# Expert weights of a soft mixture of experts: each lane loads neighbouring rows as one run of 8192 bytes, and slot inputs and ReLU results are turned from strided columns

## The chip, the core and the metric

The kernel runs on one core of a Trainium2 chip. The metric is the time of one execution on the device in microseconds (us). A core has five engines that run side by side and meet at semaphores: PE (TensorE, the matmuls; PEld is its weight load), DVE (VectorE), ACT (ScalarE), POOL (GpSimd) and SP (SyncE, which here issues nearly all transfers). The transfers themselves are carried by 16 DMA engines.

## The reference, cut to what matters

Attention with clusters comes first, then a soft mixture of eight experts (the part that is changed), then a feed-forward layer with a PReLU.

```python
def _moe_ref(x, phi, w1, w2):          # x 1536x512, w1 8x512x1024, w2 8x1024x512
    logits = x @ phi                   # 32 slots, four for each expert
    d = exp(logits - max over tokens); d /= d.sum(0) + 1e-9
    slot_input = (d.T @ x).reshape(8, 4, 512)
    for e in range(8):
        h = np.maximum(slot_input[e] @ w1[e], 0.0)      # 4x1024
        slot_out[e] = h @ w2[e]                         # 4x512
    ...
    return c @ slot_out
```

The feed-forward layer behind it is `prelu(x @ w_in) @ w_out`, with weights that arrive as 64-bit floats and are unpacked by ACT, DVE and POOL.

## The kernel before

**Stages.** From the start to about 270 us the kernel works on 16 heads of attention (lines 500 to 725: scores, exponentials, sums, products with v). Around 262 to 279 us the slots' inputs are formed (`dispatch`), from 279 to 311 us the eight experts run, and from 312 us to the end the feed-forward layer runs. An order written out by numbers (`TABLE`) decides in which order the steps of the attention are issued; the expert stage and what follows are written out as code. Each engine works through its own instructions in that order, and each transfer is issued by SP in its place in SP's order.

**Expert weights.** Each expert has four units of 1 MB: two of w1 (256 rows of 1024 floats each) and two of w2 (512 rows of 512 floats each), 32 units in all. A unit lies in one buffer of 128 lanes (partitions) by 2048 floats. `load_w` (line 239) issues the loads, all at line 248. Of units 0 to 19, which are loaded beside the attention, 18 are loaded in two halves (`half` 0 and 1) and units 15 and 19 whole; units 20 to 31 are loaded whole by `more_w`, three into `unit_we` and nine into `unit_wr`. Before the change lane p holds rows p, p+128, p+256 and so on of its unit: two runs of 4096 bytes for w1, four runs of 2048 bytes for w2.

**An expert.** `siT` holds the slots' inputs turned over (features in lanes, 32 slots in columns), made at lines 1030 to 1038: eight matmuls (four in the code, and each float32 matmul leaves two records in the trace) with a slice of `si` as stationary operand. `expert1(e)` (line 1095) multiplies `siT` with w1, 16 matmuls over 256 columns that give the 1024 hidden values as four strips of 32 lanes by 256 columns, and ACT writes them with a ReLU to `hs` (line 1105). `turn(e)` (line 1107) lets DVE turn each block of 32x32 of `hs` into `hT`, so that hidden values lie in lanes. `expert2(e)` (line 1112) multiplies `hT` with w2, eight matmuls over 512 columns. `hs` and `hT` have one buffer each, so `turn(e+1)` waits until `expert2(e)` has read `hT`. For e up to 5 the code issues `expert1(e+1)` ahead of `expert2(e)`; for e = 6 it comes behind it. `comb_step` puts four other pieces of work in between, and `warm` puts in small matmuls that compute nothing.

**Behind the experts.** The sum of the experts is turned (line 1224), multiplied with `w_in` (line 1243), and the layer's two products follow (lines 1280 and 1316 to 1318). `load_o` issues the loads of `w_out` (lines 1165 to 1174), and three parts of `w_in` come back from a scratch tensor `wsp` in DRAM (line 842), where they lie as runs of 8192 bytes for each lane.

Of the kernel before, what the change touches and what calls it, by code (L numbers as in the profile page):

```python
# [16 lines left out]
P = 128  # L17
# [97 lines left out]
def clustered_attention_soft_moe_prelu_ffn(  # L115
# [32 lines left out]
    pe, dve, act, pool, sp = nc.tensor, nc.vector, nc.scalar, nc.gpsimd, nc.sync  # L148
# [25 lines left out]
    def misc(dt=F32, hold=False):  # L174
        turns[0] = 1 - held[0] if held else 1 - turns[0]
        if hold:
            held.append(turns[0])
        return psm.tile([P, 1024 if dt == BF16 else 512], dt, name=f"misc{turns[0]}")
# [5 lines left out]
    def unit(pl, dt=F32):  # L184
        return pl.tile([P, 2048], dt, name=f"unit_{pl.name}")
# [51 lines left out]
    wts = {}  # L237

    def load_w(u, pl, half=None):
        e, i = divmod(u, 4)  # L240
        if half in (None, 0):
            wts[u] = unit(pl).rearrange("p (k f) -> p k f", k=2 if i < 2 else 4)
        t = wts[u]
        src = (w1[e, i * 256:i * 256 + 256] if i < 2 else w2[e, (i - 2) * 512:(i - 1) * 512])
        src = src.rearrange("(k p) f -> p k f", p=P)
        k = t.shape[1] // 2
        n = slice(0, 2 * k) if half is None else slice(half * k, half * k + k)
        sp.dma_start(out=t[:, n], in_=src[:, n])
# [68 lines left out]
    dsp = {}  # L317
# [526 lines left out]
    def more_w(n, pl):  # L844
        for _ in range(min(n, 32 - nxt[0])):
            load_w(nxt[0], pl)
            nxt[0] += 1
# [9 lines left out]
    for h in range(NH):  # L857
        s0, p = 6 * h, h // 2
        z = {0: "z_", NH - 1: "t_"}.get(h, "")
        ld = T["ld"][h] if h < len(T["ld"]) else 0  # L860
        for c in range(6):
# [3 lines left out]
            k = c if h == NH - 1 and c > 3 else c | 1  # L865
# [98 lines left out]
    def more_l(u, nm, half):  # L964
        if nm not in lf:
            refill(nm, *{"a": (2, early, opa), "b": (1, opb), "c": (1, opc)}[nm])
        load_w(u, lf[nm], half)
# [21 lines left out]
    for e in sorted(ev, key=lambda e: e[:2]):  # L989
        assert all(n in done or n in tags for n in e[4]), e  # L990
        wait.append(e)
        while True:
# [4 lines left out]
            _, _, f, a, need, tag = go  # L997
# [16 lines left out]
    siT = cp.tile([P, 4, 32], F32, name="siT")  # L1014
# [15 lines left out]
    for r in range(2):  # L1030
        ps = misc()
        l0 = r * 64
        for k in range(2):
            pe.matmul(
                ps[:, k * 32:k * 32 + 32], dsp["si"][l0:l0 + 64, k * P:k * P + P],
                G[l0:l0 + 64, :32], start=True, stop=True,
            )
        dve.tensor_copy(siT[:, 2 * r:2 * r + 2].rearrange("p k s -> p (k s)"), ps[:, :64])
# [55 lines left out]
    hTs = {}  # L1094
    def expert1(e):
        hp_ = ps1.tile([P, 2, 512], F32, name="s1")[:, 0, :256]
        for k in range(4):
            wa = wts[4 * e + k // 2][:, k % 2, :].rearrange("p (c f i) -> p f c i", c=8, f=4)
            for f in range(4):
                pe.matmul(  # L1100
                    hp_[f * 32:f * 32 + 32, :].rearrange("p (c i) -> p c i", c=8), siT[:, k, :],
                    wa[:, f], start=(k == 0), stop=(k == 3),
                )
        hTs[e] = hs = cp.tile([P, 256], F32, name="hs")
        act.activation(hs, hp_, AF.Relu, scale=cs[:, C_EM + e:C_EM + e + 1])

    def turn(e):
        hT = cp.tile([P, 256], F32, name="hT")
        dve.transpose(hT, hTs[e])
        hTs[e] = hT  # L1110

    def expert2(e):
# [11 lines left out]
    PIPE = T["pipe"]  # L1124
    WC, WD, WE = T["wc"]
    expert1(0)
    comb_step(0)
    more_w(2, wr)
    slopes()
    warm(wk[10])  # L1130
    turn(0)
    warm(wk[11])
    for e in range(8):
        if e < PIPE:
            expert1(e + 1)
        expert2(e)
        if PIPE <= e < 7:
            expert1(e + 1)
        if e < 7:
            turn(e + 1)  # L1140
        more_w(4, wr)
        if e in (3, 5, 6):
            comb_step((e - 1) // 2 if e < 6 else 3)
# [78 lines left out]
    ps = misc()  # L1222
# [211 lines left out]
```

## Time and profile before

| what | us |
|---|---|
| median of 3 runs | 473.07 |
| lowest and highest run | 467.2 and 473.77 |
| the profiled execution: its own time | 472.17 |
| its span, from first to last instruction | 470.4 |
| PE busy in the span | 440.7 (94%) |
| 16 DMA engines: share taken by SP's queue | 58.5% |

The span is shorter than the execution's own time by 1.8 us, which lie around it. All times in the rows below count from the span's start.

### The profile page before, as it was taken

To read this page: it belongs to the slowest core of one execution; us is meant where nothing else is said; L and a number is where in the kernel's file an instruction comes from. 1 tells how busy PE (TensorE), PEld (TensorE's weight loads), DVE (VectorE), ACT (ScalarE), POOL (GpSimd) and SP (SyncE) were. 2 spreads that over 40 slices of the span, in tenths; PEclk is the share of its full clock that TensorE was granted. 3 is DMA by queue.
4 is the path that set the end of the run, shared out by engine and by line. 5 is a ranking of instruction groups with operands and counts; after the bars stand their busy time and mean duration, and the time that the engine had idled before them with its cause. 6 is when DMAs were issued, how large, how long until landed. Compare 5 with 4: busy or idle time off the path is not lost.

```text
span 470.4 us, 8258 instructions
## 1 busy us (share of the span) xinstructions
PE 440.7 (94%) x2964; PEld 296.5 (63%) x2964; DVE 312.6 (66%) x527; ACT 289.7 (62%) x542; POOL 232.6 (49%) x277
## 2 busy tenths in 40 slices
PE   8879998999997999998999889988799999999996
PEld 5656555566564555664655444456588888888885
DVE  3777879978779477786561571337899996444442
ACT  4868597778767566685654311258898865343341
POOL 4547789878998488798988100013432330000000
PEclk9999999999999799999999999999999999999999
DMA  8796985587678559776688799998121003000003
GB/s 310 211 319 169 277 263 169 143 243 237 208 238 224 168 181 285 242 240 200 182 246 278 303 363 381 398 416 346 54 86 42 1 1 134 1 0 0 1 1 134
DMA packets 35357, 90.50 MB, mean 192 GB/s; under 512 B 5298, under 2 KB 5894, under 8 KB 34932
## 3 DMA queue, kind: packets, MB, share of 16 engines
q1 hardware_dynamic: 34884, 89.73, 58.5%
q8 instruction: 23, 0.38, 0.3%
q10 hardware_dynamic: 432, 0.24, 0.2%
q14 instruction: 18, 0.15, 0.1%
HBM read 69.57 MB, written 6.33 MB: 161 GB/s over the span
## 4 chain that ended last, share of the span: by engine, by line
PE 59%; DVE 13%; DMA 12%; issue 7%; ACT 5%; POOL 3%; SPq 1%; POOLq 0%; DVEq 0%; ACTq 0%
PE s L604 9%; PE ot L632 9%; PE ob L1317 8%; PE ob L1318 8%; PE ob L1316 8%; PE s L536 6%; DVE cs L543 4%; DMA unit_wr<-in_w_out 4%; DMA unit_wr<-in_w 3%; DMA B<-unit_wr 2%; PE hp L1280 2%; PE s L1100 1%; PE L L660 1%; ACT pt L607 1%; DMA B<-ohm 1%
## 5 line engine op out<-in xcount | busy, mean ns | idle before, releaser
L620 POOL TENSOR_TENSOR ss<-ss,pt 128x384 f32<-128x384 f32 x150 | 145.3, 1005 | 12.7 <-PE ot L632 12.5
L543 DVE TENSOR_REDUCE cs<-s 128x1 f32<-128x768 f32 x93 | 88.5, 951 | 41.9 <-PE s L536 41.5
L607 ACT ACTIVATE pt<-s 128x384 f32<-128x384 f32 x160 | 70.0, 489 | 51.3 <-PE s L604 48.9
L604 PE MATMUL s<-A,B 97*128 97x384 f32 (+1 forms) x384 | 94.9, 368 | 5.0 <-DMA B<-unit_wr 2.5
L604 PEld LDWEIGHTS s<-A,B 97*128 97x128 f32 (+1 forms) x384 | 64.3, 193 | 33.6 <-issue 17.3
L1316 PE MATMUL ob<-unit_wr,gh 128*128 128x512 f32 x192 | 75.6, 394 | 1.7 <-ACT unit_wr L1342 1.2
L1317 PE MATMUL ob<-unit_wr,gh 128*128 128x512 f32 x192 | 75.1, 391 | 1.7 <-POOL unit_wr L1208 1.7
L1318 PE MATMUL ob<-unit_wr,gl 128*128 128x512 f32 x192 | 75.1, 391 | 0.0
L1208 POOL TENSOR_TENSOR unit_wr<-unit_wr 128x256 fp32r<-128x256 f32 x32 | 24.9, 801 | 86.2 <-ACT unit_wr L1201 83.7
L632 PE MATMUL ot<-pt,raw_v 128*64 128x384 f32 x320 | 63.1, 507 | 0.0
L536 PE MATMUL s<-B,A 96*128 96x384 f32 x192 | 53.9, 363 | 7.2 <-DVE cs L543 4.9
L1302 DVE SCALAR_TENSOR_TENSOR g<-hp,sal,hs 128x768 f32<-128x768 f32 (+1 forms) x34 | 32.8, 968 | 27.4 <-ACT hs L1300 27.3
L1300 ACT ACTIVATE hs<-hp,sgn 128x768 f32<-128x768 f32 (+1 forms) x34 | 29.1, 861 | 27.0 <-PE hp L1280 26.7
L536 PEld LDWEIGHTS s<-B,A 96*128 96x128 f32 x192 | 32.7, 192 | 19.8 <-DVE cs L543 16.2
L1316 PEld LDWEIGHTS ob<-unit_wr,gh 128*128 128x128 f32 x192 | 36.0, 188 | 9.1 <-ACT unit_wr L1342 1.6
L1317 PEld LDWEIGHTS ob<-unit_wr,gh 128*128 128x128 f32 x192 | 36.1, 188 | 8.7 <-POOL unit_wr L1208 2.4
L1318 PEld LDWEIGHTS ob<-unit_wr,gl 128*128 128x128 f32 x192 | 36.1, 188 | 8.1 <-DVE gl L1306 0.3
L1306 DVE TENSOR_TENSOR gl<-g,gh 128x768 fp32r<-128x768 f32 (+1 forms) x34 | 30.8, 911 | 15.4 <-ACT gh L1304 15.3
L1304 ACT ACTIVATE gh<-g 128x768 fp32r<-128x768 f32 (+1 forms) x34 | 27.3, 805 | 18.3 <-DVE g L1302 18.1
L632 PEld LDWEIGHTS ot<-pt,raw_v 128*64 128x64 f32 x320 | 20.0, 138 | 24.0 <-issue 23.3
L698 POOL TENSOR_TENSOR unit_wr<-unit_wr,tr 128x192 f32<-128x192 f32 x13 | 7.7, 593 | 34.6 <-DVE tr L696 34.6
L797 POOL TENSOR_TENSOR unit_wr<-unit_wr 128x256 uint32<-128x256 uint32 x32 | 22.5, 730 | 2.8 <-DVE unit_wr L790 2.8
(198 smaller groups left out, 611.8 us busy)
## 6 DMA issues: line engine op xcount, KB each, us to landing
unit_wr<-in_w SPq DMA_DIRECT2D x30, 512.0 KB
unit_wr<-in_w SPq DMA_DIRECT2D x9, 1024.0 KB
unit_wr<-in_w_in SPq DMA_DIRECT2D x16, 512.0 KB
unit_wr<-in_w_out SPq DMA_DIRECT2D x5, 1024.0 KB
unit_wr<-in_qn SPq DMA_DIRECT2D x8, 384.0 KB
unit_wr<-in_qT SPq DMA_DIRECT2D x8, 384.0 KB
unit_wr<-in_kn SPq DMA_DIRECT2D x8, 384.0 KB
unit_wr<-in_kT SPq DMA_DIRECT2D x8, 384.0 KB
```

The costliest lines, as they stand in the source:

```text
L536: pe.matmul(ps[hf], a[:96, c * P:c * P + P], b[:96, hf * 384:hf * 384 + 384], start=True, stop=True,)
L543: dve.tensor_reduce(m, t, axis=AX.XY, op=ALU.max, negate=True)
L604: pe.matmul(ps[:, :384], b[:, c * P:c * P + P], a[:, hs], start=(i == 0), stop=(i == 1))
L607: act.activation(e[:, hs], ps[:, :384], AF.Exp, scale=0.125)
L620: (pool if h < T["sp"] else dve).tensor_tensor(ss[h][:, hs], ss[h][:, hs], sme[h, c][:, hs], op=ALU.add)
L632: pe.matmul(ot[h][hf * 64:hf * 64 + 64, :], v[:, c, par * 64:par * 64 + 64], e[:, hf * 384:hf * 384 + 384], start=(c == 0), stop=(c == 5),)
L1300: act.activation(hs, hv, AF.Copy, scale=sgn[:, f:f + 1])
L1302: dve.scalar_tensor_tensor(g, hv, sal[:, f:f + 1], hs, op0=ALU.mult, op1=ALU.max)
L1306: dve.tensor_tensor(gl, g, gh.bitcast(F32), op=ALU.subtract)
L1316: pe.matmul(ob[t], gh[:, c], wh(f), start=(f == 0), stop=False)
L1317: pe.matmul(ob[t], gh[:, c], wlo(f), start=False, stop=False)
L1318: pe.matmul(ob[t], gl[:, c], wh(f), start=False, stop=(f == 15))
```

## The change

Lane p now takes neighbouring rows: rows 2p and 2p+1 of a unit of w1, rows 4p to 4p+3 of a unit of w2. A whole unit is then one run of 8192 bytes in each lane. A half keeps a run of 4096 bytes for w1 and gets one of 4096 bytes, in place of two of 2048, for w2. The features that lie in lane p are thereby others, so two operands are reordered to match: the slice of `si` that makes `siT` takes every second column (`k:k + 255:2`) in place of 128 neighbouring ones, and `turn` reads `hs` in each 32x32 block with a step of four floats (16 bytes) and writes `hT` as before. The view of w1 in `expert1` has two runs of 128 columns for each matmul in place of eight runs of 32.

```diff
@@ load_w @@
         src = (w1[e, i * 256:i * 256 + 256] if i < 2 else w2[e, (i - 2) * 512:(i - 1) * 512])
-        src = src.rearrange("(k p) f -> p k f", p=P)
+        src = src.rearrange("(p k) f -> p k f", p=P)
@@ siT @@
-                ps[:, k * 32:k * 32 + 32], dsp["si"][l0:l0 + 64, k * P:k * P + P],
+                ps[:, k * 32:k * 32 + 32], dsp["si"][l0:l0 + 64, k:k + 255:2],
@@ expert1 @@
-            wa = wts[4 * e + k // 2][:, k % 2, :].rearrange("p (c f i) -> p f c i", c=8, f=4)
+            wa = wts[4 * e + k // 2][:, k % 2, :].rearrange("p (c f i) -> p f c i", c=2, f=4)
             for f in range(4):
                 pe.matmul(
-                    hp_[f * 32:f * 32 + 32, :].rearrange("p (c i) -> p c i", c=8), siT[:, k, :],
+                    hp_[f * 32:f * 32 + 32, :].rearrange("p (c i) -> p c i", c=2), siT[:, k, :],
                     wa[:, f], start=(k == 0), stop=(k == 3),
@@ turn @@
-        dve.transpose(hT, hTs[e])
+        dve.transpose(
+            hT.rearrange("p (c g s) -> p c g s", c=2, g=4),
+            hTs[e].rearrange("p (c i g) -> p c g i", c=2, g=4),
+        )
```

No instruction is added, removed or moved on any engine; only the shapes of transfers and operands differ. The place where this shows is SP's list of transfers at the end of the attention and in the expert stage. In the rows, `unit_wr`, `unit_wc` and `unit_we` are buffers of weight units by their pools, `in_w` is w1 or w2, `in_w_out` is the output weight of the feed-forward layer, and the lines of the changed kernel are higher by 3 from `turn` on.

```order
-L248 DMA unit_we<-in_w 128x2x1024 x2
-L248 DMA unit_we<-in_w 128x4x512
-L248 DMA unit_wr<-in_w 128x4x512
-L248 DMA unit_wr<-in_w 128x2x1024 x2
-L248 DMA unit_wr<-in_w 128x4x512 x2
-L248 DMA unit_wr<-in_w 128x2x1024 x2
-L248 DMA unit_wr<-in_w 128x4x512 x2
-L1165 DMA unit_wr<-in_w_out 128x1024
+L248 DMA unit_wr<-in_w 128x1024 x2
+L248 DMA unit_wc<-in_w 128x2048
+L248 DMA unit_we<-in_w 128x2048 x3
+L248 DMA unit_wr<-in_w 128x2048 x9
```

Nothing moved: the same twelve whole units (3 + 9) stand in the same order ahead of the first load of `w_out`, and their shapes 128x2x1024 and 128x4x512 have become 128x2048, one run for each lane, the shape that the three loads from `wsp` at line 842 have before and after the change. The first two lines with a plus stand for the last halves and for unit 19, whose lines with a minus lie above this piece.

## Rows read from the trace of the kernel before

**Rows 1.** The page's head: span and busy time of each engine.
```profile
span 470.4 us, 8258 instructions
PE 440.7 (94%) x2964; PEld 296.5 (63%) x2964; DVE 312.6 (66%) x527; ACT 289.7 (62%) x542; POOL 232.6 (49%) x277
```

**Rows 2.** The chain that ended last, expert stage: start us, length us, what.
```profile
285.20 1.73 PE s L1100 x32
286.93 1.03 PE L L1118 x9
287.97 15.84 DMA unit_wr<-in_w
...
303.87 18.42 DMA unit_wr<-in_w_out
322.29 0.02 issue
322.31 1.03 ACT hs L1300 x2
```

**Rows 3.** Busy time by stretch: bounds, length, engines, granted clock, DMA share, GB/s.
```profile
220.00:262.00 42.00, 40.45 (x263) 23.99 (x256) 20.69 (x40) 22.59 (x51) 34.24 (x38) 1.00 0.80 243
262.00:279.00 17.00, 14.30 (x148) 8.07 (x148) 11.26 (x37) 3.78 (x10) 0.59 (x1) 1.00 0.85 328
279.00:312.00 33.00, 32.35 (x418) 15.01 (x419) 8.73 (x25) 8.19 (x18) 0.00 (x0) 1.00 1.02 386
312.00:345.00 33.00, 27.25 (x226) 20.56 (x225) 25.84 (x41) 27.24 (x51) 12.25 (x18) 1.00 0.57 224
345.00:400.00 55.00, 55.00 (x249) 46.06 (x248) 48.77 (x60) 41.85 (x63) 15.72 (x20) 1.00 0.13 49
```

**Rows 4.** Waits from 279 to 345 us: who for whom, us, times, longest.
```profile
PE ob L1317 <- POOL unit_wr L1208: 1.7, 2, 1.3
PE hp L1280 <- ACT unit_wr L1201: 1.4, 1, 1.4
PE ob L1316 <- ACT unit_wr L1342: 1.2, 1, 1.2
PE hp L1280 <- ACT unit_wr L1257: 1.0, 1, 1.0
DVE unit_wr L1229 <- DMA unit_wr<-wsp: 0.7, 1, 0.7
PEld L L1118 <- DMA unit_wr<-in_w: 0.3, 1, 0.3
```

**Rows 5.** DMA packets, 300.4 to 302.9 us: runs of 2048 bytes.
```profile
DMA packets 487, 0.97 MB, mean 388 GB/s; under 512 B 15, under 2 KB 15, under 8 KB 487
q1 hardware_dynamic: 487, 0.97, 104.6%
```

**Rows 6.** DMA packets, 295.2 to 297.9 us: runs of 4096 bytes.
```profile
DMA packets 279, 1.08 MB, mean 401 GB/s; under 512 B 15, under 2 KB 15, under 8 KB 279
```

**Rows 7.** DMA packets, 307.2 to 309.8 us: runs of 8192 bytes.
```profile
DMA packets 152, 1.09 MB, mean 419 GB/s; under 512 B 17, under 2 KB 17, under 8 KB 21
```

**Rows 8.** Groups by shape on DVE: count, busy us, mean ns, idle before.
```profile
L1109 DVE STREAM_TRANSPOSE hT<-hs 128x256 f32<-128x256 f32 x8 | 3.6, 444 | 20.0 <-PE L L1118 15.6 <-ACT hs L1105 4.3
L667 DVE STREAM_TRANSPOSE tr<-L 128x192 f32<-128x192 f32 x16 | 6.1, 378 | 2.6 <-PE L L688 2.3 <-PE L L660 0.3
L736 DVE TENSOR_REDUCE unit_wr<-misc 1x32 f32<-1x128 f32 x2 | 0.6, 278 | 0.4 <-PE misc L734 0.4
L732 DVE TENSOR_REDUCE ml<-unit_wr 128x1 f32<-128x192 f32 x2 | 0.7, 347 | 0.0
L673 DVE RECIPROCAL rin<-rs 128x6 f32<-128x6 f32 x16 | 3.1, 192 | 0.5
L382 DVE RECIPROCAL rn<-n 128x24 f32<-128x24 f32 x8 | 2.1, 286 | 1.2 <-ACT n L369 0.6 <-POOL B L272 0.5
```

**Rows 9.** Order of time, 281 to 283.5 us, DVE and then PE.
```profile
281.53 0.45 DVE L1109 STREAM_TRANSPOSE hT<-hs 128x256 f32<-128x256 f32 x1
...
281.55 1.93 PE L1100 MATMUL s<-unit_wr,siT 128*32 128x256 f32 x32 [0.59 <-ACT hs L1105]
283.31 0.61 PE L1118 MATMUL L<-unit_wr,hT 128*32 128x512 f32 x4
```

**Rows 10.** Order of time, 302 to 312 us, DVE and then PE.
```profile
302.79 0.45 DVE L1109 STREAM_TRANSPOSE hT<-hs 128x256 f32<-128x256 f32 x1 [3.20 <-PE L L1118]
307.51 0.45 DVE L1109 STREAM_TRANSPOSE hT<-hs 128x256 f32<-128x256 f32 x1 [4.28 <-ACT hs L1105]
...
303.29 1.92 PE L1118 MATMUL L<-unit_wr,hT 128*32 128x512 f32 x16
...
308.01 1.06 PE L1118 MATMUL L<-unit_wr,hT 128*32 128x512 f32 x8
...
311.36 0.62 PE L1224 MATMUL misc<-G,sob 128*128 128x32 f32 x4
```

**Rows 11.** Groups by shape on PE, PEld and ACT: operands, slices, weights.
```profile
L1100 PE MATMUL s<-unit_wr,siT 128*32 128x256 f32 x208 | 12.6, 380 | 0.9 <-ACT hs L1105 0.6 <-DVE siT L1038 0.3
L1118 PE MATMUL L<-unit_we,hT 128*32 128x512 f32 x8 | 1.0, 592 | 0.0
L1243 PE MATMUL ob<-unit_wr 128*32 128x128 f32 x128 | 4.1, 275 | 0.1
L1034 PEld LDWEIGHTS misc<-G,unit_wr 64*128 64x128 f32 x8 | 0.5, 186 | 0.5 <-DVE unit_wr L771 0.5
L779 ACT ACTIVATE unit_wr<-unit_wr 128x512 uint32<-128x512 uint32 x32 | 21.4, 669 | 0.1
L1201 ACT ACTIVATE unit_wr<-unit_wr 128x512 fp32r<-128x512 f32 x16 | 10.0, 626 | 2.2 <-DVE unit_wr L797 1.9
```

**Rows 12.** Waits of the whole span that name a DMA, PE's own.
```profile
PE s L604 <- DMA B<-unit_wr: 2.5, 2, 1.6
```

**Rows 13.** DMA queue of SP, whole span: packets, MB, share of 16 engines.
```profile
q1 hardware_dynamic: 34884, 89.73, 58.5%
```

## The prediction

> **What bounds the kernel now.** I read the page's head first. PE is busy for 440.7 of 470.4 us [rows 1], so any gain has to come out of the 30 us in which PE is idle, or out of PE's own work. The chain that ended last names something else for the expert stage: from 287.97 us it runs through a load of expert weights (15.84 us) and, without a break, a load of `w_out` (18.42 us) until 322.29 us [rows 2]. That is 34 us in which transfers seem to set the end, and the change makes just these transfers shorter.
>
> The table by stretch says how to take that. From 279 to 312 us the DMA engines are full (share 1.02, 386 GB/s), but PE is busy for 32.35 of 33.00 us in the same stretch [rows 3]. Two resources are full side by side, and the chain, which knows only one path, went along the DMA. What PE could gain there is 0.65 us. The list of waits from 279 to 345 us tells the same from the other side: among PE's waits the transfers stand with one entry, 0.3 us of a weight load in `expert2`; the long ones behind 312 us (1.7, 1.4, 1.2 and 1.0 us) are for POOL and ACT, which split the weights of the feed-forward layer [rows 4]. DVE waits for a transfer once, 0.7 us at line 1229, ahead of a copy of what PE makes at line 1224; PE's own row there starts at 311.36 us and lasts 0.62 us, to 311.98 us [rows 10], so the copy at 312 us would have to wait for PE anyway. From 345 us on PE is busy without a gap (55.00 of 55.00), so whatever is gained or lost before 345 us reaches the end one for one.
>
> So the kernel is bound by PE in the expert stage, and by small waits on ACT and POOL behind it. The weights arrive in time.
>
> **The change part by part.**
>
> *The loads.* The trace has all three run lengths in stretches that hold hardly anything else: 2048 bytes at 388 GB/s (w2 now) [rows 5], 4096 bytes at 401 GB/s (w1 now) [rows 6] and 8192 bytes at 419 GB/s (the loads from `wsp`, which have the shape that whole units get) [rows 7]. The small packets counted under 512 bytes carry no weight. A unit is 1.0486 million bytes: 2.70, 2.61 and 2.50 us. A whole unit of w2 gains 0.20 us of the DMA engines' time, one of w1 0.11 us, a half of w2 0.04 us (from 2048 to 4096 bytes, 0.085 us for a unit), a half of w1 nothing. Units 20 to 31 are whole, six of each kind: 6 x 0.20 + 6 x 0.11 = 1.9 us. Units 15 and 19 are whole w2: 0.4 us. Eight units of w2 in halves: 0.7 us, spread over the attention. In sum 3.0 us of DMA time, of which 1.9 us lie where the DMA engines are full. What hides it is PE's 32.35 us of work: the last weights come 1.9 us earlier to an engine that does not wait for them. Without that cover it would be worth the 1.9 us. I take 0 for the whole units; the bounds are 0 and -2.3 us.
>
> In the attention the small moves between buffers stand in SP's queue behind the halves. PE waits for such a move twice, 2.5 us together [rows 12]. A half of w2 ahead of it is 0.04 us shorter, or two of them 0.1 us. I take -0.1 us; the far bound is the 0.7 us.
>
> *The turn.* Eight transposes of 444 ns each [rows 8]. The same instruction over 192 columns takes 378 ns, so a column costs 66/64 = 1.03 ns and the rest, 180 ns, is fixed. The instruction now reads every fourth float. For a read with a wide step the nearest row is line 736, which reduces 128 values of one partition that lie 32 floats apart: 278 ns. The reductions of line 732 lie side by side, 192 values in 347 ns; at 1.03 ns a value, 128 of them would take 281 ns. The wide step costs nothing there, though it reads the matmuls' result memory. I take 444 ns as before. For the far bound I use the dearest value in DVE's rows: the reciprocal at line 382, which goes through its 24 values in a changed order, takes 94 ns more than 6 values at line 673, 5.2 ns for each of the 18. At that price a turn takes 180 + 256 x 5.2 = 1510 ns, 1.07 us longer.
>
> [...]
>
> Where would a slower turn be felt? The first ends at 281.98 us and its reader starts at 283.31 us [rows 9]: 1.33 us to spare. Turns 1 to 5 run beside the next expert's first product, 32 records of PE in 1.73 us [rows 2], so 1.28 us to spare. Turn 6 ends at 303.24 us and PE begins to use it at 303.29 us; turn 7 ends at 307.96 us and is used at 308.01 us [rows 10]. These two have 0.05 us. Up to 1.07 us longer, six turns of eight cost nothing, and the last two 2 x (1.07 - 0.05) = 2.0 us. Value taken 0, bounds 0 and +2.0 us.
>
> *The slice of si.* Eight weight loads of 186 ns [rows 11] now read with a step of 8 bytes. ACT's unpacking at line 779 has the same step: 669 ns for 512 values against 626 ns for a plain copy at line 1201, 7% more. That would be 8 x 186 x 0.07 = 0.1 us, at a place where nothing covers it. Value 0, bounds 0 and +0.1 us.
>
> *The view of w1.* Matmuls over 128, 256 and 512 columns take 275, 380 and 592 ns [rows 11], 0.82 and 0.83 ns a column. Only the middle one reads runs of 32 floats, and it lies on the line of the others. Short runs cost nothing before, and longer runs give nothing back. No instruction is added, and none changes its place.
>
> **The sum.** 472.17 us (the profiled execution's own time, 470.4 in the span) - 0.1 = 472.1 us. The median of the runs is 473.07 us, 0.9 us above the profiled execution, and the runs lie between 467.2 and 473.77 us: this spread of 6.6 us is larger than every term above.
>
> **The rivals.**
>
> *The transfers do set the end.* For it: the chain [rows 2] and a DMA share of 1.02. Against it: 0.3 us of waiting for weights [rows 4]. Then the 1.9 us and the 0.4 us come through, and the 0.7 us of the attention: 472.2 - 3.0 = 469.2 us. It is worth more than my forecast as soon as a wait of PE behind 312 us turns out to hang on when a transfer landed. All those waits together are 5.3 us, so even this case stays within 2%.
>
> *The strided turn is slow (slower than before).* For it: 256 reads, each four floats from the last, and no row that reads this memory so. Against it: line 736. It decides from the point where a turn takes more than 0.49 us (444 ns and the 0.05 us to spare); at twice its time it adds 2 x (0.44 - 0.05) = 0.8 us, at the far bound 2.0 us, and from 1.72 us on the six others are felt too. With the slice's 0.1 us: 473.0 to 474.3 us. [...]
>
> *The change doesn't do what it says.* The transfers could be cut into packets of the old length. The loads from `wsp` speak against it: the same shape moves 1.09 MB in 152 packets, of which 131 have 8192 bytes [rows 7]. The time would be 472.2 us.
>
> **How the numbers follow.** The forecast (covered transfers, turns at their old price) has 0.58, the transfers 0.20, the slow turn 0.14, the old packets 0.03; 0.05 remain for something that no row shows. Faster or slower by over 2% means 9.4 us, about what a measurement of this kernel can tell from no change; no named case reaches it, so only the rest and the spread of the runs speak for it: faster 0.05, within 2% 0.90, slower 0.05. The range holds the rivals' ends, 469.2 and 474.3 us, and the spread of the runs below and above: from 467.2 us, the fastest run of before, to 475.2 us, the slow end plus the 0.9 us by which the median lies above the profiled execution.
>
> **What would show it right or wrong.** In the trace of after: packets of 8192 bytes and more than 410 GB/s while whole units are loaded; SP's queue with some 3 us less of the 16 engines' time (58.5% of the span [rows 13] would become 57.9%); line 1109 (or its new number) at 444 ns, and six turns without a waiting PE; PE's idle time from 279 to 312 us still near 0.65 us and from 312 to 345 us near 5.7 us. My prediction is wrong if that idle time behind 312 us shrinks together with the transfers, or if PE waits for the turns of experts 6 and 7, or if the attention, which I left alone, moves by more than the runs do.

## The result and the profile after

The changed kernel takes 475.31 us, the median of 20 runs (470.21 to 478.61); the kernel before, run beside it 20 times, takes 470.86 us (467.2 to 474.9). The ratio is 1.0082, interval [1.0059, 1.0104]: slower by some 3.9 us. Ratios and intervals (95%) in this document leave out the slow runs, those more than 1.5% above the fastest of their kernel (here the 478.61 us; never more than two of a kernel). The loss is less than 2%, as forecast, but it is not the forecast "no change", and the median lies 0.1 us above the range.

The two profiled executions hide it. The one of before took 472.17 us, high among its runs; the one of after took 472.23 us, low among its runs, and both have a span of 470.4 us [rows 1]. Laid side by side they show where single pieces of work grew, but their difference is not the difference of the kernels. That has to come from more traces, below.

The page's head and SP's queue, after:

```profile
span 470.4 us, 8258 instructions
PE 439.9 (94%) x2964; PEld 295.7 (63%) x2964; DVE 314.7 (67%) x527; ACT 289.7 (62%) x542; POOL 232.6 (49%) x277
...
q1 hardware_dynamic: 28996, 89.73, 58.4%
```

Only DVE's busy time moved by more than a microsecond (312.6 to 314.7). SP's queue moves the same 89.73 MB in 28996 packets in place of 34884, and takes 58.4% in place of 58.5% of the engines' span [rows 13]; the forecast was 57.9%. In microseconds of all 16 engines that is 274.7 in place of 275.2, a gain of 0.5 where 3 were forecast. The whole units alone (e4, below) did gain what they were to gain, so something else took it back.

Busy time by stretch, after (columns as in [rows 3]):

```profile
262.00:279.00 17.00, 14.74 (x160) 8.32 (x163) 11.21 (x38) 3.35 (x9) 0.60 (x1) 1.00 0.81 319
279.00:312.00 33.00, 31.79 (x413) 14.60 (x406) 9.99 (x23) 8.08 (x18) 0.00 (x0) 1.00 1.01 412
312.00:345.00 33.00, 27.26 (x227) 20.59 (x227) 25.74 (x41) 27.26 (x51) 12.24 (x18) 1.00 0.48 189
345.00:400.00 55.00, 55.00 (x249) 46.05 (x248) 48.83 (x60) 41.91 (x62) 15.74 (x20) 1.00 0.13 49
```

In the expert stage (second row) the transfers run at 412 in place of 386 GB/s, as forecast, and PE is idle for 1.21 us in place of 0.65: the faster loads bought nothing, and something else takes 0.6 us. The stage can also be taken from its first product (line 1100) to the turn of the sum (line 1224, after 1227). Before, then after:

```profile
279.03 1.93 PE L1100 MATMUL s<-unit_wr,siT 128*32 128x256 f32 x32 [0.30 <-DVE siT L1038]
...
311.00 0.53 PE L1224 MATMUL misc<-G,unit_wr 128*128 128x32 f32 x4
```

```profile
278.52 1.93 PE L1100 MATMUL s<-unit_wr,siT 128*32 128x256 f32 x32 [0.31 <-DVE siT L1038]
...
311.11 0.53 PE L1227 MATMUL misc<-G,unit_wr 128*128 128x32 f32 x4
```

That is 31.97 us before and 32.59 us after. Behind 312 us PE is busy for 27.26 us as before (27.25), although the transfers land earlier. So they did not set the end there.

The turn, after: its durations (ns: lowest, median, highest), then who waited for it (us in total, times).

```profile
L1109 DVE STREAM_TRANSPOSE hT<-hs x8: 634/666/700, 281.0 to 307.4; 128x256 f32<-128x256 f32 x8
...
who waited for it (us, times):
  PEld L L1121: 0.8, 2
  PE L L1121: 0.4, 2
```

666 ns in place of 445 (mean 444 in [rows 8]), half as much again, for the same 256 columns: read with a step of 16 bytes, the turn takes 0.22 us more than the 0.445 us it took before. The prediction had the slow turn as a rival with a chance of 0.14, and this trace agrees with that rival.

PE in the order of time, after, against [rows 10]; the bracket is PE's idle time and what ended it:

```profile
298.73 1.93 PE L1100 MATMUL s<-unit_wr,siT 128*32 128x256 f32 x32 [0.25 <-ACT hs L1105]
...
303.21 1.92 PE L1121 MATMUL L<-unit_wr,hT 128*32 128x512 f32 x16 [0.18 <-DVE hT L1109]
...
308.13 1.06 PE L1121 MATMUL L<-unit_wr,hT 128*32 128x512 f32 x8 [0.17 <-DVE hT L1109]
```

The last two are the places that the prediction named (turns 6 and 7). The first is a third one that it missed. Before the change PE went into the same product without a wait:

```profile
299.00 1.93 PE L1100 MATMUL s<-unit_wr,siT 128*32 128x256 f32 x32
```

The chain that ended last shows its way, after:

```profile
295.17 0.68 DVE hT L1109
295.85 0.44 DVE csm L1055
...
296.78 0.57 DVE cx L1058
...
297.81 0.51 ACT unit_wr L1064
298.31 0.37 ACT hs L1105
298.68 0.04 issue
298.73 1.93 PE s L1100 x32
```

Turn 4 has 1.3 us to spare for its own reader, but `comb_step` has queued the softmax of the combine weights behind it on DVE; ACT waits for that at line 1064, the next expert's ReLU stands behind line 1064 on ACT, and PE waits for the ReLU. So the turn is felt three times, about 0.2 us each.

PE's waits that name a small move between buffers, over the whole span, after (before there was the first kind alone, 2.5 us [rows 12]):

```profile
PE s L604 <- DMA B<-unit_wr: 3.0, 3, 1.8
PE s L536 <- DMA B<-ohm: 1.2, 1, 1.2
```

The attention, which I had left alone, waits 1.7 us more for transfers, at a place (line 536) where it did not wait before.

### The profile page after: what moved, and what is told of

Read it like the earlier page. It is cut to its first block, busy times and chain, and to the rows that moved or that the text cites. A ratio compares the mean times of both kernels' runs of the same rounds, so it can differ in the third digit from the quotient of the medians.

```text
span 470.4 us, 8258 instructions
## 1 busy us (share of the span) xinstructions
PE 439.9 (94%) x2964; PEld 295.7 (63%) x2964; DVE 314.7 (67%) x527; ACT 289.7 (62%) x542; POOL 232.6 (49%) x277
## 3 DMA queue, kind: packets, MB, share of 16 engines
q1 hardware_dynamic: 28996, 89.73, 58.4%
## 4 chain that ended last, share of the span: by engine, by line
PE 61%; DVE 12%; DMA 10%; issue 7%; ACT 4%; POOL 4%; SPq 1%; POOLq 0%; DVEq 0%; ACTq 0%
PE ot L632 9%; PE s L604 9%; PE ob L1320 8%; PE ob L1321 8%; PE ob L1319 8%; PE s L536 5%; DMA B<-unit_wr 4%; DVE cs L543 4%; PE s L1100 3%; PE L L1121 3%; PE hp L1283 2%; DMA unit_wr<-in_w_out 2%; DMA md<-ohm 1%; POOL ss L620 1%; DMA B<-ohm 1%
```

## The experiments

The kernels that change only part of the whole (the turn alone, any of the loads alone) take rows or hidden values in an order that their other operands don't match; so they do not compute the reference's output, and their times are what they are for. All ratios are against the kernel before, run in the same job.

**The parts, each alone.** The turn:

```diff
-        dve.transpose(hT, hTs[e])
+        dve.transpose(
+            hT.rearrange("p (c g s) -> p c g s", c=2, g=4),
+            hTs[e].rearrange("p (c i g) -> p c g i", c=2, g=4),
+        )
```

> The kernel before with the strided turn alone; loads, the slice of si and the view of w1 stay as they were, so the hidden values meet the wrong rows of w2 and the output is not the reference's. Theory turn (the strided transposes cost the time, in the expert stage or by what they delay): ratio to before 1.006 to 1.010, some 3 to 5 us. Theory attention (the loads cost it): turns of 0.67 us as in the profile after, expert stage 0.6 us longer, ratio 1.001 to 1.002.

Measured 1.0049 [1.0024, 1.0073], between the two ranges, with turns and an expert stage as the second theory had them. Once more:

> The strided turn alone in the kernel before, once more, with the same change of the result as in its first run. If the turn costs what the expert stage of the traces shows, 0.6 us: ratio 1.000 to 1.003. If it costs what the first run gave: 1.003 to 1.007.

Measured 1.0024 [0.9996, 1.0052], as the 0.6 us of the trace would have it. The traces are sharper than the run times: from the first product of expert 0 to the turn of the sum the kernel before takes 31.97 us, both of these take 32.60.

The loads, all of them, then the halves alone, then the whole units alone:

```diff
-        src = src.rearrange("(k p) f -> p k f", p=P)
+        src = src.rearrange("(p k) f -> p k f", p=P)                                          # e2
+        src = src.rearrange("(k p) f -> p k f" if half is None else "(p k) f -> p k f", p=P)  # e3
+        src = src.rearrange("(p k) f -> p k f" if half is None else "(k p) f -> p k f", p=P)  # e4
```

> The kernel before with the new row order in all 32 loads alone; siT, the view of w1 and the turn stay, so rows and features do not match and the output is not the reference's. Theory attention: ratio 1.006 to 1.010, with longer waits for the small moves in the attention stage. Theory turn: ratio 0.997 to 1.000.

Measured 1.0076 [1.0049, 1.0103], as the theory of the attention has it.

> The kernel before with the new row order only in the 18 units that are loaded in halves beside the attention (runs of 4096 bytes for w1 as before but from every second row, 4096 in place of 2048 for w2); units 15 and 19 to 31 as before; the output is not the reference's. Theory halves (the halves hold up the small moves behind them): ratio 1.006 to 1.009, nearly all of the loss. Theory whole units: 0.999 to 1.001.

Measured 1.0074 [1.0045, 1.0103], as the theory of the halves has it.

> The kernel before with the new row order only in the 14 units that are loaded whole (15, 19 and 20 to 31: runs of 8192 bytes); halves as before; the output is not the reference's. Theory whole units (runs of 8192 bytes late in the attention or in the expert stage cost the time): ratio 1.005 to 1.009. Theory halves: 0.996 to 1.000, with shorter loads in the expert stage and no gain on PE.

Measured 1.0018 [0.9988, 1.0048], in neither range but not told apart from 1, with 415 GB/s from 279 to 312 us and the same 31.97 us of expert stage as before. SP's queue:

```profile
q1 hardware_dynamic: 31044, 89.73, 58.1%
```

Of the span of 467.6 us that is 271.7 us, against 274.0 us (58.6% of 467.5) in the kernel before as run again (e11) and 275.2 us in its first trace: the 2.3 us of DMA time forecast for the whole units are there. They are worth nothing to the kernel, as forecast, and the halves carry nearly all that the loads cost.

**Which halves, and why.** In w1 a half keeps its runs of 4096 bytes, but they were neighbours and now every second one is left out. In w2 the run grows from 2048 to 4096 bytes, and between the runs 4096 bytes are left out. e5 takes the new order for the halves of w1 alone, e6 for those of w2 alone:

```diff
-        src = src.rearrange("(k p) f -> p k f", p=P)
+        src = src.rearrange("(p k) f -> p k f" if half is not None and i < 2 else "(k p) f -> p k f", p=P)   # e5
+        src = src.rearrange("(p k) f -> p k f" if half is not None and i >= 2 else "(k p) f -> p k f", p=P)  # e6
```

> The kernel before with the new row order only in the 10 units of w1 that are loaded in halves. The run length stays 4096 bytes; only the source differs: a half reads every second run of 4096 bytes of its unit in place of 512 KB in one piece. The output is not the reference's. Theory source (a half that reads every second 4 KB comes slower, and the small moves behind it land later): ratio 1.002 to 1.006, and the halves of w1 take over 2 us each where they took some 1.5. Theory run length (it is the longer packets of w2's halves that hold up the queue): 0.998 to 1.001.

Measured 1.0006 [0.9974, 1.0038]: in the range of the run's length, and against the gaps. Its trace is of its longest execution (474.55 us) and is left out of the table further down. Once more:

> Only the halves of w1 with gaps, once more; the output is not the reference's. The first run showed loads as slow as in the changed kernel and no loss of time. If the slow loads of w1 are at places that nothing waits for: 0.998 to 1.002. If the first run was chance: 1.003 to 1.006.

Measured 1.0032 [1.0003, 1.0061]: this time in the other range. Together the two leave some 0.2% for the gaps in w1, hardly clear of nothing.

> The kernel before with the new row order only in the 8 units of w2 that are loaded in halves: runs of 4096 bytes in place of 2048, each half from every second 4 KB. The output is not the reference's. Theory source: ratio 1.002 to 1.005. Theory run length: 1.005 to 1.009, nearly all that the halves together cost.

Measured 1.0045 [1.0013, 1.0078], in the range of the gaps ("source"). Then the halves of w2 with runs of 4096 bytes, but each half one unbroken piece:

```diff
+        if half is not None and i >= 2:
+            sp.dma_start(
+                out=t[:, half * 2:half * 2 + 2],
+                in_=src[half * 256:half * 256 + 256].rearrange("(p k) f -> p k f", p=P),
+            )
+            return
```

> The kernel before, where each half of a w2 unit is read in runs of 4096 bytes (two neighbouring rows for each lane) from 512 KB in one piece; w1 and whole units as before; the output is not the reference's. It has the run length of the run with all halves changed without its gaps in the source. Theory source: ratio 0.997 to 1.001. Theory run length: 1.003 to 1.009.

Measured 1.0011 [0.9984, 1.0039], just above the range of the gaps and below that of the run's length. This and e6 are the clean pair: the same units, the same runs of 4096 bytes, with and without gaps, in one job. The means of their runs differ by 1.6 us, give or take 1.5. So most of what the w2 halves cost goes with the gaps; a small cost of the run's length is not excluded. Two kernels with all operands in matching order followed. e8 is the changed kernel with the reorder moved to ACT's ReLU, so that the turn reads in line; e9 does the same and leaves no gaps (w1 as before, w2 in unbroken pieces of 512 KB):

```diff
-        act.activation(hs, hp_, AF.Relu, scale=cs[:, C_EM + e:C_EM + e + 1])
+        act.activation(
+            hs.rearrange("p (c g i) -> p c i g", c=2, g=4),     # e9: c=4, g=2
+            hp_.rearrange("p (c i g) -> p c i g", c=2, g=4),
+            AF.Relu, scale=cs[:, C_EM + e:C_EM + e + 1],
+        )
...
-        src = src.rearrange("(p k) f -> p k f", p=P)            # e9 alone, for w2
+        src = src.rearrange("(h p g) f -> p h (g f)", h=2, p=P)
+        t = t.rearrange("p (h g) f -> p h (g f)", h=2)
```

> The changed kernel, where the ReLU on ACT writes its 256 columns in the order that the turn needs, so that the turn reads neighbouring floats again; it computes the reference's result. If the strided turn costs only what the expert stage shows (0.6 us): ratio to before 1.0065 to 1.0075, turns back at 0.44 us, ACT's ReLU at 0.47 us or a little more. If the turn costs what its run alone showed (0.49%): 1.003 to 1.005.

Measured 1.0066 [1.0037, 1.0095], in the first range, but not for its reason, as the ReLU shows below.

> A version of the change without gaps in the source and without a strided turn: w1 as before; each half of a w2 unit is 512 KB in one piece in runs of 4096 bytes, in whole units as well; the ReLU on ACT writes the order that the turn needs. It computes the reference's result. Theory gaps (halves that read every second 4 KB hold up the attention): ratio 0.998 to 1.001, loads of the halves no longer than before, and no gain from the shorter loads either, since PE does not wait for them. Theory run length: 1.003 to 1.008.

Measured 1.0049 [1.0017, 1.0082], against 0.998 to 1.001: a miss. Its trace says why. The ReLU of e8, its duration in ns (before: 471 on the mean):

```profile
L1105 ACT ACTIVATE hs<-s,cs x8: 697/710/722, 281.9 to 308.3; 128x256 f32<-128x256 f32 x8
```

And the one of e9, whose write goes to and fro between two strips in place of four:

```profile
L1109 ACT ACTIVATE hs<-s,cs x8: 703/716/727, 278.5 to 305.0; 128x256 f32<-128x256 f32 x8
```

The turn went back to 445 ns and the ReLU rose by 240 ns on the same path: the expert stage takes 32.69 us in both. I had moved the cost, not removed it: that e8 came out in its range was luck, and e9 holds a slow reorder beside loads that cost nothing; it does not speak against the gaps.

**Loads by themselves.** e10 adds, in the feed-forward stage, twelve loads of 512 KB to a tile of their own, each behind the last: in turns one unbroken piece and every second 4096 bytes; the last six each have a move of 192 KB ahead.

> The kernel before with twelve loads of 512 KB added in the feed-forward stage, where the queue is nearly idle, each into a spare buffer that the next one waits for: in turn one that reads 512 KB in one piece and one that reads every second 4 KB of 1 MB, both in runs of 4096 bytes; the last six behind a move of 192 KB between two buffers. Nothing reads them. If gaps alone make a load slower: 0.4 to 1.5 us longer each with gaps than without. If it takes the attention's other traffic: the same time within 0.2 us, some 3 us each.

The issues of the last six in e10 (start us; each waits until the one before has landed, so the step is its time). The first is in one piece, the second has gaps, and so on:

```profile
371.57 0.33 SPq L1365 DMA_DIRECT2D dmy<-in_w  x1
...
375.27 0.33 SPq L1365 DMA_DIRECT2D dmy<-in_w  x1
...
379.60 0.33 SPq L1365 DMA_DIRECT2D dmy<-in_w  x1
...
383.61 0.33 SPq L1365 DMA_DIRECT2D dmy<-in_w  x1
...
387.21 0.33 SPq L1365 DMA_DIRECT2D dmy<-in_w  x1
...
390.48 0.33 SPq L1365 DMA_DIRECT2D dmy<-in_w  x1
```

Beside each of these a move runs. One piece: 3.70, 4.01 and 3.27 us; with gaps: 4.33 and 3.60 us. Without a move ahead, from the same list, one piece took 3.33 and 3.20 us, with gaps 3.99 and 3.51 us. On the mean 3.86 us with gaps against 3.50 us in one piece, and the two sets overlap (the load with gaps issued at 367.19 us, beside which the first move runs, took 4.38 us and is not in the mean): inconclusive, it points the same way. One core in a quiet stage is not the attention's queue.

**What stayed open after these, in one job.** Every part had read above 1. The kernel before against itself:

> The kernel before, unchanged: what two equal kernels read against each other in one job. Theory A (the small ratios above 1 of the parts are real): 1.000 with 1 inside the interval, within 0.998 to 1.002. Theory B (a kernel that is placed beside the runs of before reads a few tenths of a per cent high by itself): 1.002 to 1.004, and then whole units alone (1.0018), the w1 halves (1.0006 and 1.0032) and the turn alone (1.0049 and 1.0024) are worth nothing.

Measured 1.0004 [0.9976, 1.0031]. The comparison itself adds nothing that can be seen within 0.3%.

> The halves in the new row order and nothing else, a second time. Theory A (the loads of halves that read one run of 4096 bytes and leave the next out hold up the attention's own small loads, and TensorE waits for these): 1.005 to 1.009, as the first time (1.0074), with waits of TensorE for B or ohm loads of 3.5 us or more beside the 2.5 us of before. Theory B (chance): 0.998 to 1.003.

Measured 1.0066 [1.003, 1.0102], as the first theory has it; its trace has 5.0 us of waits for these moves.

> Only the w2 halves, each lane taking two neighbouring rows (runs of 4096 bytes), but each half one unbroken piece of the source; its result is wrong by row order, its loads are what it is for. Theory A (what the source leaves out between the runs costs, not the run's length): 0.999 to 1.002, like the first time (1.0011), below the halves alone in the same job by 0.3 per cent or more. Theory B (any change of the halves' packets shifts the attention's loads and costs the same): equal to the halves alone within 0.2 per cent.

Measured 1.0016 [0.9987, 1.0045]: below the halves alone by 0.5%, as the gaps would have it. The comparison is not a clean one, since the halves alone have gaps in w1 too; e6 and e7 are. Last, the changed kernel without gaps and with a turn whose read steps over two floats in place of four:

```diff
-            hT.rearrange("p (c g s) -> p c g s", c=2, g=4),
-            hTs[e].rearrange("p (c i g) -> p c g i", c=2, g=4),
+            hT.rearrange("p (c g s) -> p c g s", c=4, g=2),
+            hTs[e].rearrange("p (c i g) -> p c g i", c=4, g=2),
```

(w1, the slice of `si` and the loads as in e9.)

> The changed kernel with w1 as before and w2 in runs of 4096 bytes, halves in one unbroken piece, so that the turn's read steps over 8 bytes and not 16. Theory A (halves without gaps cost nothing; a turn whose read strides costs on the path of the experts): the turn between 445 and 664 ns if the cost goes with the stride, about 550 ns, and 1.001 to 1.003. If the turn takes 660 ns at 8 bytes too, any stride costs the same and the ratio is that of the turn alone, 1.002 to 1.005. Theory B (the halves cost with or without gaps): 1.006 to 1.009.

Measured 1.0024 [0.999, 1.0057]. The turn of e14, in ns:

```profile
L1113 DVE STREAM_TRANSPOSE hT<-hs x8: 439/446/457, 276.8 to 302.8; 128x256 f32<-128x256 f32 x8
```

446 ns against 445 before: here a step of 8 bytes costs nothing, where one of 16 bytes costs 0.22 us. I had expected about 550. Why the price comes in between the two steps no run here shows. The expert stage of e14 takes 31.98 us, that of before. So the loss of the turn can be designed away, and that of the halves for the most part; what is left is not told apart from the kernel before, and not faster. No version here beats it.

## Why the prediction was wrong, point by point

**The first reading stood.** PE bounds the expert stage and the transfers are covered: e4 gives the whole units 415 GB/s and the stage does not move from 31.97 us. The rival that the transfers set the end (0.20) is refuted by this, and so is the one that the packets stay old (0.03): SP's queue has 28996 packets in place of 34884. Of the signs of being wrong that the prediction had named, that one did not come (PE is idle for 5.74 us from 312 to 345 us, before 5.75). The two others did: PE waits for the turns of experts 6 and 7, and the attention moved.

**The step that failed is the halves in the attention.** I sized it from the run's length alone: nothing for w1, -0.04 us for each half of w2, -0.1 us in sum, far bound -0.7. The diff said more: with two or four neighbouring rows to a lane, a half reads 4096 bytes and leaves the next 4096 out. No row of before showed a source with gaps, and I gave this term no bound on the side of a loss. The traces of the experiments show its size. Every trace has the first product of expert 0 (line 1100, or its new number), which ends the attention; two of them, from the last job. The kernel before again (e11):

```profile
276.20 1.93 PE L1100 MATMUL s<-unit_wr,siT 128*32 128x256 f32 x32 [0.30 <-DVE siT L1038]
```

The halves alone again (e12):

```profile
281.43 1.93 PE L1100 MATMUL s<-unit_wr,siT 128*32 128x256 f32 x32 [0.30 <-DVE siT L1038]
```

The same row of all traces but that of e5:

| halves read | traces | first product at, us | mean | PE waits for `B` moves, mean us |
|---|---|---|---|---|
| in one piece | before, e1, e1b, e4, e7, e9, e10, e11, e13, e14 | 274.27 to 279.81 | 276.8 | 2.5 |
| with gaps | after, e2, e3, e5b, e6, e8, e12 | 277.77 to 281.43 | 279.4 | 4.4 |

(The waits are the entries `PE s <- DMA B<-unit_wr` and `B<-ohm` of each trace, summed; the second kind stands in five of the seven with gaps and in none of the other ten.) The attention ends 2.6 us later with gaps, on the mean; the two sets overlap, and give or take 1.4 us is a fair estimate from their spread. Runs of 4096 bytes without gaps (e7, e9, e13, e14) stand in the first row with a mean of 277.0 us, the six kernels with the halves of before with one of 276.7 us, so the run's length does not show here. The halves of w1, whose run did not change (e5b, 280.63 us; e5 281.45 us), stand with the second row, but both traces are of executions over 3 us longer than the mean of their kernel's runs, and by run times their loss is small (1.0006 and 1.0032). Behind the first product all traces agree to 0.2 us, but for the turn or the reordering ReLU.

The loss is there without any fall of the clock. e3 had a mean granted clock of 1.00 over its whole execution, and its row and its waits for transfers are:

```profile
278.95 1.93 PE L1100 MATMUL s<-unit_wr,siT 128*32 128x256 f32 x32 [0.30 <-DVE siT L1038]
```

```profile
PE s L604 <- DMA B<-unit_wr: 3.0, 3, 1.9
PE s L536 <- DMA B<-ohm: 2.1, 2, 1.8
```

The traces without gaps at that clock (e1, e4, e14) have the row at 275.58, 276.28 and 274.27 us, with 3.0, 1.9 and 2.0 us of such waits: the attention of e3 ends 3.6 us later than their mean, and PE waits 2.8 us more for these moves.

How it comes through can be read in e12. PE there, in the order of time:

```profile
150.68 0.44 PE L604 MATMUL s<-A,B 97*128 97x384 f32 x1
154.21 1.30 PE L604 MATMUL s<-A,B 128*128 128x384 f32 x3 [3.09 <-DMA B<-unit_wr]
155.30 0.84 PE L536 MATMUL s<-B,A 96*128 96x384 f32 x2
156.07 2.83 PE L632 MATMUL ot<-pt,raw_v 128*64 128x384 f32 x8
```

The same products in e11:

```profile
150.20 1.09 PE L604 MATMUL s<-A,B 97*128 97x384 f32 x4
151.31 0.62 PE L536 MATMUL s<-B,A 96*128 96x384 f32 x2
151.87 1.51 PE L632 MATMUL ot<-pt,raw_v 128*64 128x384 f32 x8
```

The move's issue by SP, in e12 and then in e11:

```profile
144.87 0.84 SPq L146 DMA_DIRECT2D B<-unit_wr  x1
```

```profile
143.93 0.92 SPq L146 DMA_DIRECT2D B<-unit_wr  x1
```

In both kernels the last transfers issued ahead of it are a half of a unit and three of 192 KB. In e12 it is issued 0.9 us later and lands later still; PE stands for 3.09 us, and the granted clock falls: the next eight records of line 632 take 2.83 in place of 1.51 us. By stretch in e12, columns as before:

```profile
140.00:152.00 12.00, 10.36 (x74) 6.36 (x72) 11.74 (x22) 10.51 (x21) 9.62 (x12) 1.00 0.90 233
152.00:158.80 6.80, 4.59 (x13) 2.23 (x13) 2.93 (x4) 2.44 (x4) 4.59 (x6) 0.57 0.26 62
```

The granted clock is 1.00 in the first stretch and 0.57 on the mean in the second. This is one example and not a mark of the gaps: in the first trace of before PE waits at the same place, for less, and the clock falls there too.

```profile
152.23 1.30 PE L604 MATMUL s<-A,B 128*128 128x384 f32 x3 [1.64 <-DMA B<-unit_wr]
```

Do the packets take longer? The traces hold the time of every packet. Among those of 4096 bytes that SP's queue moves in the first 262 us, the mean is 182 to 190 ns in the six kernels with the halves of before, and 193 and 195 ns with gaps in w1 alone (e5, e5b). Where the w2 halves have runs of 4096 bytes too, it is 188 to 192 ns without gaps (e7, e9, e13, e14) and 194 to 198 ns with them (e6, e3, e12, e2, e8, after). The packets of 3072 bytes, which the small moves use, stand at 173 to 177 ns in all. So loads with gaps do take longer, but by little: 5 ns on some 6400 packets are, by estimate, 2 us of the 16 engines' time over the whole attention. Why so little makes single moves land microseconds late was not separated from other orders of landing (e10 is inconclusive), and stays open.

**The strided turn.** Taken as 0, because line 736 reads with a wide step at no cost (278 ns, against 281 ns estimated for values side by side); that row reads what PE wrote (`misc`, lines 734 and 736) and not `hs`, as the text itself said, and the cost was 0.22 us. The rival was right that the strided turn is slow (666 ns in place of 444), and the point from which it decides (0.49 us) was passed. Its price by the text's own sum would be 2 x (0.666 - 0.444 - 0.05) = 0.34 us; measured 32.60 - 31.97 = 0.63 us, because turn 4 was costed by its reader alone and not by what stands behind it on DVE. The bound of +2.0 us held. The rival's whole time, 473.0 to 474.3 us, missed all the same, because it too left the halves at nothing.

**The slice of `si`.** 192 in place of 186 ns, eight times: 0.05 us, inside the bound of 0.1.

**The sum as it came out.** 2.6 us for the halves and 0.6 us for the turn make 3.2 us; measured 3.9 us, interval 2.8 to 4.9. By the ratios of e2 (all loads), e3 and e12 (1.0066 to 1.0076 of some 468 us) the loads are 3.1 to 3.6 us, which with the turn is the whole. These are the two terms that I had set at -0.1 and 0. No rival named the larger one, and the range was drawn without it. The base of the sum hid part of the miss: the profiled execution of before (472.17 us) lies 1.3 us above the median of the 20 runs (470.86 us).

## What to carry to other kernels

When rows are given out anew to the lanes, look at what a partial load leaves out of its source and not only at the length of its runs (with gaps the attention ended 2.6 us later here, on the mean), and try small urgent transfers ahead of such loads in the queue (no run here tried it); for whole units the longer run was worth nothing here, since PE was the bound (e4: 415 GB/s, and 31.97 us of expert stage as before). A read with a step of 16 bytes was not free on DVE (666 ns in place of 445, +50%), one of 8 bytes was (446 ns); ACT's ReLU lost as much (710 and 716 ns in place of 471, +51 and +52%) when it wrote with a step of 32 floats, to four strips or to two. Cost a slower instruction by everything queued behind it on its engine, and test a small effect with the unchanged kernel beside it in the same job.

## What the runs showed that I had not expected

The time of a run hangs in good part on whether the granted clock fell somewhere in it. In the last job 28 of 35 runs of before kept a mean granted clock of at least 0.998 and took 468.3 us on the mean; the other seven took 470.6 us. The halves alone (e12) kept it in 6 of 12 runs, at 469.7 us, and took 473.8 us in the others; the changed kernel kept it in 2 of 20 runs (470.21 and 470.83 us). So the halves with gaps cost about 1.4 us in runs at full clock, and a run in which the clock falls is longer by 2.3 us (before) to 4.2 us (e12). That falls become more frequent by the gaps is not shown: without gaps, in the same job, e13 kept the clock in 5 of 12 runs (468.6 us) and e14 in 4 of 12 (468.1 us). At full clock these two are within 0.4 us of the kernel before. The profiled execution of before was itself one with a fall (152.0 to 158.8 us), so it was a poor yardstick for a change of 1%:

```profile
152.00:158.80 6.80, 6.57 (x20) 4.07 (x20) 2.44 (x3) 3.88 (x8) 4.03 (x6) 0.50 0.23 64
```

Twenty records of PE fill 6.57 us there, at half the clock; in e11, whose clock is 1.00 there, the same stretch holds 61.
